# Favor attention and a feed-forward network on one core: the order of all engines, planned anew with measured durations

## The chip, the cores and the metric

The kernel runs on one core of one Trainium2 chip. The metric is the device time of one execution in microseconds (us). Before the change it is 939.01 us, the median of 3 runs (938.88 to 939.64).

## The reference

For 8 batches of 8 heads, 576 positions and head width 64, linear attention with 128 random features; its output, 4608 tokens by 512, goes through a feed-forward network 512 to 2048 to 512:

```python
def phi(x):
    proj = np.einsum('bhsd,md->bhsm', x, omega)
    h = proj - np.sum(x * x, axis=-1, keepdims=True) / 2.0
    return np.exp(h - np.max(h, axis=-1, keepdims=True)) / np.sqrt(m)
q_p, k_p = phi(q_s), phi(k_s)
kv, z = np.einsum('bhsm,bhsd->bhmd', k_p, v), np.sum(k_p, axis=2)
attn = np.einsum('bhsm,bhmd->bhsd', q_p, kv) / (np.einsum('bhsm,bhm->bhs', q_p, z)[..., None] + 1e-06)
x = attn.transpose(0, 2, 1, 3).reshape(B * S, H * D)
h = x @ w_in
out = (0.5 * h * (1.0 + erf(h / sqrt(2)))) @ w_out
```

## The kernel before, in words

**Attention.** The heads of a batch go in pairs, 4 units per batch, 32 in all. The first 8 units are computed in fp32, the 24 later ones from a high and a low part (`split_pre`, `split_post`). A unit's high part `r` is written by ScalarE (`x_high`, L979), and GpSimd writes the low part beside it (`x_low`, L984); both feed TensorE's projections (L992). Each batch has one scale group for v (`v_scales`, on GpSimd) that `v_a` and `v_b` need.

**Network.** The tokens go in 18 blocks of 256. Block 0 is plain fp32. In blocks 1 to 17 the first product is a Strassen-like scheme of seven products on fp16 high and low parts: `sw1` and `sw2` (`product`, L1264) for each of 8 chunks of hidden units, with the sums between by `comb_a` on ScalarE (L1271) and `comb_b`, `comb_c` on VectorE (L1276, L1277, L1282). Then `gelu` (L1290) and `g_high` (L1299) on ScalarE and `g_low` (L1364, writes `gl`) on VectorE, and the second product (`ffn_second`, L1374 to L1376) into `acc`; `o` leaves it by L1381 and L1383. In half of block 15 and in 16 and 17 the second product is Strassen-like too; its weight sums come late (`weights_out_sums`: L638, L649 on VectorE, L643 on GpSimd, L646 on ScalarE).

**Scales of a block.** Before a block's input can be split, `block_scales` computes its scale on GpSimd: six instructions of 32 x 1 elements (L505, L506, L507, L1215, L1216, L500), each needing one ahead of it. Blocks that span two batches take `be` from VectorE first (L1208). `block_spread` (L510, L511, ScalarE) copies the scale to the other partitions. Then `t_sum` (L1233, GpSimd, writes `ts`), `block_high` (L1243, ScalarE, writes `xh`) and `block_low` (L1246, VectorE, writes `xl`), four parts each, make what the block's products read. `gelu`, `g_high` and `g_low` read the scale tile too.

**The order.** All of it is decided when the program is built. Every step is an `op(engine, cost, function, ...)` with a planned duration in us. The class `Planner` (L234; its `run`, L280) plays the whole program through: whenever an engine is free in the plan, it takes, among the steps that are ready in the plan and have a buffer, the one with the lowest number in the table `RANK` (L37). The planner also keeps apart VectorE steps in the set `PORT` and steps of GpSimd. The order so found is fixed on each engine. Where the plan has TensorE waiting for more than 0.9 us, `put` (L1569) issues fill matmuls (L1574), whose result is overwritten:

```python
if X['fill'] and o.idle > 0.9 and o.t > 5.0:
    t = [G[k] for (_, k), name in zip(o.new, o.pick) if name in ANY]
    for _ in range(int((o.idle - 0.3) * X['fill'] / 0.11) if t else 0):
        nc.tensor.matmul(t[0][:, 0:256], id16[:, 0:P], id16, start=True, stop=True)
```

On the chip an engine runs its list in order and waits wherever an input is late, whatever the plan held.

Of the kernel before, what the change touches and what calls it, by code (L numbers as in the profile page):

```python
# [36 lines left out]
RANK = (0, 0, 0, 0, 0, 1, 2, 1, 4, 5, 1, 3, 1, 4, 2, 4, 7, 4, 5, 9, 8, 10, 9, 7, 13, 25, 28, 3, 10, 14, 12, 16, 13, 17, 17, 23, 19, 24, 22, 30, 23,  # L37
# [357 lines left out]
def favor_attention_ffn(ctx: ExitStack, tc: tile.TileContext, qT, kT, v, omT, w_in, w_out, out):  # L395
    nc = tc.nc
    B, H, D, S = qT.shape
    NJ = H // 2
    M = omT.shape[1]
    DM, F = w_in.shape  # L400
# [8 lines left out]
    NT = R2 // P  # L409
# [13 lines left out]
    cp = ctx.enter_context(tc.tile_pool(name="cp", bufs=1))  # L423
# [43 lines left out]
    op = PL.op  # L467
# [1145 lines left out]
```

## Time and profile before

| what | value |
|---|---|
| median of 3 runs | 939.01 us (938.88 to 939.64) |
| the profiled execution's own time | 938.51 us |
| its span | 936.5 us |
| mean granted TensorE clock | 0.995 |
| TensorE busy | 98% of the span |
| VectorE, ScalarE, GpSimd busy | 84%, 81%, 59% |
| DMA | 76 GB/s in the mean |

PE is TensorE's matmuls, PEld its weight loads (beside the matmuls), DVE VectorE, ACT ScalarE, POOL GpSimd. A row of a timeline gives start, duration, engine, line, operation, output<-input and size, and in brackets how long the engine stood idle just before and who released it. `[2.04 <-POOL bs L500]` reads: 2.04 us idle, ended when GpSimd's L500 had written `bs`. A row of the windows view gives the stretch, its length, busy time and count of PE, PEld, DVE, ACT and POOL, the granted clock of TensorE (1.00 is 2.4 GHz, 0.50 is 1.2 GHz), the busy share of DMA and its GB/s. A row of the waits view gives who waited for whom: total us, times, longest.

### The profile page before, as it was taken

What the parts mean: (1) busy time and instruction counts of PE and PEld (TensorE: products, weight loads), DVE (VectorE), ACT (ScalarE), POOL (GpSimd) and SP (SyncE); (2) the same over time, 40 slices, a digit from 0 to 9 for tenths busy, and PEclk for the clock granted to TensorE, in tenths of its full rate; (3) what the DMA queues carried; (4) which work ended last, traced back from release to release, by engine and by line L of the source; (5) the groups of instructions that cost most, each with busy time, mean ns of one, the idle gap of its engine ahead of it and who ended that gap; (6) DMA issues with size and microseconds to landing.
All of it is one profiled execution on the core that took longest, in us unless ns stands there. A gap on an engine that the chain in (4) does not pass through costs nothing.

```text
span 936.5 us, 26349 instructions
## 1 busy us (share of the span) xinstructions
PE 919.4 (98%) x10171; PEld 716.9 (77%) x10171; DVE 789.9 (84%) x2160; ACT 754.7 (81%) x1660; POOL 550.9 (59%) x809
## 2 busy tenths in 40 slices
PE   8999999999999999999999999999999999899998
PEld 7996777687767777777777777777777777679997
DVE  3777899999988998888988998899888998778764
ACT  5998988789979887979779897888898876657544
POOL 0454657747567664955466755674768744865432
PEclk8999999999999999999999999999999999999999
DMA  8884314033223232211221232112321100000000
GB/s 243 247 261 157 132 52 133 27 92 88 77 52 89 60 95 66 85 44 49 67 89 42 85 94 63 53 52 77 78 75 53 48 2 24 2 24 2 24 13 34
DMA packets 46316, 71.48 MB, mean 76 GB/s; under 512 B 13680, under 2 KB 22256, under 8 KB 46192
## 3 DMA queue, kind: packets, MB, share of 16 engines
q1 hardware_dynamic: 45824, 69.19, 24.7%
q8 instruction: 80, 1.31, 0.6%
q10 hardware_dynamic: 368, 0.62, 0.2%
q14 instruction: 44, 0.36, 0.1%
HBM read 60.36 MB, written 9.44 MB: 75 GB/s over the span
## 4 chain that ended last, share of the span: by engine, by line
PE 72%; DVE 12%; ACT 7%; POOL 4%; issue 2%; DMA 2%; SPq 1%; DVEq 0%; POOLq 0%; ACTq 0%
PE h L1264 25%; PE acc L1374 8%; PE acc L1375 8%; PE acc L1376 8%; PE h L1251 3%; PE acc L1367 3%; PE at L992 2%; PE at L1014 2%; PE at L1077 2%; PE at L864 2%; PE acc L1329 2%; PE at L1329 2%; DVE w L1067 1%; DVE h L1277 1%; DVE gl L1364 1%
## 5 line engine op out<-in xcount | busy, mean ns | idle before, releaser
L984 POOL TENSOR_TENSOR r<-xt,r 64x288 fp32r<-64x288 f32 (+2 forms) x216 | 164.8, 776 | 115.4 <-ACT r L979 85.8
L1264 PE MATMUL h<-xh,w 128*128 128x128 f16 x2176 | 219.5, 219 | 0.0
L1264 PE MATMUL h<-xl,w 128*128 128x128 f16 x1088 | 200.0, 219 | 0.0
L1264 PEld LDWEIGHTS <-w 128*128 128x128 f16 x3264 | 196.5, 98 | 4.5 <-issue 0.6
L1374 PE MATMUL acc<-woh,gh 128*128 128x512 f16 x448 | 170.5, 380 | 1.0 <-ACT o L1381 1.0
L1375 PE MATMUL acc<-woh,gl 128*128 128x512 f16 x448 | 170.0, 379 | 0.7 <-DVE gl L1364 0.6
L1376 PE MATMUL acc<-wol,gh 128*128 128x512 f16 x448 | 169.9, 379 | 0.0
L1264 PE MATMUL h<-xh,wih 128*128 128x128 f16 x816 | 156.9, 220 | 4.9 <-DVE gl L1364 2.5
L1264 PE MATMUL h<-xh,wil 128*128 128x128 f16 x816 | 156.1, 219 | 0.0
L1264 PE MATMUL h<-xl,wih 128*128 128x128 f16 x816 | 156.1, 219 | 0.0
L1264 PEld LDWEIGHTS <-wih 128*128 128x128 f16 x1632 | 139.3, 98 | 15.6 <-DVE h L1282 4.4
L1364 DVE SCALAR_TENSOR_TENSOR gl<-h,bs,gh 128x512 f16<-128x512 f32 x116 | 86.2, 744 | 18.9 <-ACT gh L1299 18.3
L1290 ACT ACTIVATE h<-h,bs 128x512 f32<-128x512 f32 x116 | 76.4, 660 | 24.7 <-PE h L1264 20.5
L979 ACT CAST r<-xt 128x256 fp32r<-128x256 f32 (+2 forms) x216 | 82.2, 407 | 8.2 <-PE at L992 3.5
L1264 PEld LDWEIGHTS <-wil 128*128 128x128 f16 x816 | 80.0, 98 | 10.1 <-issue 3.6
L1376 PEld LDWEIGHTS <-gh 128*128 128x128 f16 x464 | 45.4, 98 | 54.5
L1299 ACT ACTIVATE gh<-h,bs 128x512 f16<-128x512 f32 x116 | 79.8, 690 | 7.8 <-PE acc L1376 5.3
L1271 ACT COPY g<-h 128x256 f32<-128x256 f32 x136 | 50.4, 371 | 32.8 <-PE h L1264 30.6
L1375 PEld LDWEIGHTS <-gl 128*128 128x128 f16 x464 | 45.5, 98 | 37.4 <-DVE gl L1364 1.4
L1374 PEld LDWEIGHTS <-gh 128*128 128x128 f16 x464 | 45.3, 98 | 37.1
L1277 DVE TENSOR_TENSOR h<-h,g 128x256 f32<-128x256 f32 x136 | 58.8, 433 | 4.7
L589 POOL TENSOR_TENSOR w<-w 128x1024 int32<-128x1024 int32 x12 | 28.6, 2385 | 56.4 <-DVE w L583 25.9
(258 smaller groups left out, 2457.9 us busy)
## 6 DMA issues: line engine op xcount, KB each, us to landing
xt<-in_qT SPq DMA_DIRECT2D x56, 288.0 KB, 3.8
xt<-in_kT SPq DMA_DIRECT2D x54, 288.0 KB, 4.1
out_x<-o SPq DMA_DIRECT2D x35, 256.0 KB, 2.5
raw<-in_w_in SPq DMA_DIRECT2D x16, 512.0 KB, 5.8
raw<-in_w_out SPq DMA_DIRECT2D x16, 512.0 KB, 4.5
w<-in_v SPq DMA_DIRECT2D x24, 320.0 KB, 3.1
vt<-in_v SPq DMA_DIRECT2D x8, 320.0 KB, 5.1
xt<-in_kT ACTq DMA_DIRECT2D x2, 288.0 KB, 3.9
```

Of the source, the lines that this page charges most:

```text
L979: nc.scalar.copy(G['r', u, x][:, 0:b - a], xf[:, a:b])
L984: nc.gpsimd.tensor_tensor(r, xf[D:, a:b], r, op=ALU.subtract)
L1264: nc.tensor.matmul(h, w[p], x[r], start=first and i + m == 0, stop=last and i == 1 and m == 2, skip_group_check=True)
L1271: nc.scalar.copy(G['sa', n, c], G['h', n, c][:, 0:2 * P])
L1277: nc.vector.tensor_tensor(hv[:, 1:3], hv[:, 1:3], q.unsqueeze(1).broadcast_to([P, 2, P]), op=ALU.add)
L1290: nc.scalar.activation(h, h, AF.Gelu, scale=G['bs', n][:, 2:3])
L1299: nc.scalar.activation(G['gh', n, c], G['h', n, c], AF.Copy, scale=G['bs', n][:, 3:4])
L1329: nc.tensor.matmul(acc, a[x], b[y], start=first and m == 0, stop=False, skip_group_check=True)
L1364: nc.vector.scalar_tensor_tensor(G['gl', n, c], G['h', n, c], G['bs', n][:, 3:4], G['gh', n, c], op0=ALU.mult, op1=ALU.subtract)
L1374: nc.tensor.matmul(acc, gh, woh[:, f, c0:c1], start=f == 0, stop=False, skip_group_check=True)
L1375: nc.tensor.matmul(acc, gl, woh[:, f, c0:c1], start=False, stop=False, skip_group_check=True)
L1376: nc.tensor.matmul(acc, gh, wol[:, f, c0:c1], start=False, stop=f == NF - 1, skip_group_check=True)
```

## The change

It changes two things. The planned durations of some 27 steps are set to other values; the six-instruction scale group goes from 0.9 to 1.7 us, the group for v from 0.9 to 1.5. And the table `RANK` is another one. No step is added or taken out, and what each computes stays. Fill matmuls follow from the plan: 16 before, all at the program's start; 19 after, 15 at the start and 4 in the tail. The diff, cut to its core:

```diff
-RANK = (0, 0, 0, 0, 0, 1, 2, 1, 4, 5, 1, 3, 1, 4, 2, 4, 7, 4, 5, 9, 8, 10, 9, 7, 13, 25,
+RANK = (0, 0, 0, 0, 0, 1, 2, 1, 2, 5, 1, 3, 1, 4, 2, 2, 5, 4, 5, 9, 8, 10, 9, 6, 11, 10,
...
-        op('ACT', 1.14, w_hi, pc, w=[rk + ('hi',)], r=[rk])
-        op('ACT', 1.2, w_lo, pc, r=[rk], w=pc.lk if pc.l is not None else [rk + ('lo',)])
+        op('ACT', 1.04, w_hi, pc, w=[rk + ('hi',)], r=[rk])
+        op('ACT', 1.05, w_lo, pc, r=[rk], w=pc.lk if pc.l is not None else [rk + ('lo',)])
...
-        op('POOL', 0.9, v_scales, b, r=[('exp', b, 0)], new=[('vsc', ('vsc', b))])
+        op('POOL', 1.5, v_scales, b, r=[('exp', b, 0)], new=[('vsc', ('vsc', b))])
...
-                op('POOL', 0.2 + m / 455, x_low, u, x, r=xr, w=[rk])
+                op('POOL', 0.22 + m / 455, x_low, u, x, r=xr, w=[rk])
...
-        op('DVE', 1.06, v_b, u, r=[u.vk, ('vsc', u.b)], w=['vb'])
+        op('DVE', 0.81, v_b, u, r=[u.vk, ('vsc', u.b)], w=['vb'])
...
-        op('POOL', 0.9, block_scales, n, r=[('be', n), ('exp', b0, 1), ('wsc', 1)], new=[('bs', ('bs', n))], kind='B')
+        op('POOL', 1.7, block_scales, n, r=[('be', n), ('exp', b0, 1), ('wsc', 1)], new=[('bs', ('bs', n))], kind='B')
...
-        op('POOL', 0.21, block_out, n, r=[('bs', n), ('wsc', 0)], w=[('bo', n)])
+        op('POOL', 0.31, block_out, n, r=[('bs', n), ('wsc', 0)], w=[('bo', n)])
...
-            op('DVE', 0.31 + m / 940, block_low, n, p, r=[('bs', n), ('xh', n), ('xh', n, p)] + (ts or xr) + xt[1:] * (p > 0), w=[('xl', n, p)],
+            op('DVE', 0.12 + m / 940, block_low, n, p, r=[('bs', n), ('xh', n), ('xh', n, p)] + (ts or xr) + xt[1:] * (p > 0), w=[('xl', n, p)],
...
-        op('DVE', 0.65, comb_b, n, c, r=[('sa', n, c)], w=[hk], new=[('g', ('qs', n, c))], kind='F')
+        op('DVE', 0.77, comb_b, n, c, r=[('sa', n, c)], w=[hk], new=[('g', ('qs', n, c))], kind='F')
...
-        op('ACT', 0.66, g_high, n, c, r=[('bs', n), hk], new=[('gh', ('gh', n, c))], kind='F')
-        op('DVE', 0.71, g_low, n, c, r=[('bs', n), hk, ('gh', n, c)], new=[('gl', ('gl', n, c))], kind='F')
+        op('ACT', 0.6, g_high, n, c, r=[('bs', n), hk], new=[('gh', ('gh', n, c))], kind='F')
+        op('DVE', 0.66, g_low, n, c, r=[('bs', n), hk, ('gh', n, c)], new=[('gl', ('gl', n, c))], kind='F')
```

The other changed durations are of the same kind, most of them by 0.1 to 0.25 us. The order moves on all engines; three places follow. A number behind a name is that of the buffer and differs between the two programs.

**First place: GpSimd, where the scales of blocks 4 and 5 are made.** Before (`bs_4049` is block 4's scale, `bs_4075` block 5's, `vsc_4119` that of v for the next batch, `r_4145` a unit's low part):

```order
L500 TENSOR_SCALAR bs_4075<-bs_4075 32x1
L1224 TENSOR_TENSOR bs_4049<-bs_4049,wsc_81 128x1
L1224 TENSOR_TENSOR bs_4075<-bs_4075,wsc_81 128x1
L505 TENSOR_SCALAR vsc_4119<-vexp_80 32x1
L506 TENSOR_SCALAR vsc_4119<-vsc_4119 32x1
L507 TENSOR_SCALAR vsc_4119<-vsc_4119 32x1
L500 TENSOR_SCALAR vsc_4119<-vsc_4119 32x1 x2
L1233 TENSOR_TENSOR ts_4134<-xs_865 128x256
L1233 TENSOR_TENSOR ts_4134<-xs_865,ts_4134 128x256
L984 TENSOR_TENSOR r_4145<-xt_82,r_4145 64x256
```

After (`bs_4059` is block 4's scale; block 5's group follows only after the last row):

```order
L500 TENSOR_SCALAR bs_4059<-bs_4059 32x1
L1233 TENSOR_TENSOR ts_4105<-xs_883 128x256
L1233 TENSOR_TENSOR ts_4105<-xs_883,ts_4105 128x256 x2
L984 TENSOR_TENSOR r_4129<-xt_82,r_4129 64x256
L1233 TENSOR_TENSOR ts_4105<-xs_883 128x256
L505 TENSOR_SCALAR vsc_4165<-vexp_80 32x1
L506 TENSOR_SCALAR vsc_4165<-vsc_4165 32x1
L507 TENSOR_SCALAR vsc_4165<-vsc_4165 32x1
L500 TENSOR_SCALAR vsc_4165<-vsc_4165 32x1 x2
L984 TENSOR_TENSOR r_4179<-xt_82,r_4179 64x256
L984 TENSOR_TENSOR r_4185<-xt_82,r_4185 64x128
L984 TENSOR_TENSOR r_4183<-xt_82,r_4183 64x256
```

Three groups in a row have become one, then sums and a low part, then the group of v; block 5's group has moved behind three more low parts.

**Second place: ScalarE in the tail, around the scales of the last two blocks.** Before (`bs_12833` is block 14's scale, `bs_14530` block 17's):

```order
L1299 ACTIVATE gh_14483<-h_14323,bs_12833 128x512
L890 COPY xs_13532<-at_14459 128x64
L890 COPY xs_13532<-at_14402 128x64
L1271 COPY g_14496<-h_14371 128x256
L646 CAST w32_71<-et_83 128x1024
L510 COPY bs_14530<-bs_14530 32x5
L511 COPY bs_14530<-bs_14530 64x5
L1290 ACTIVATE h_14371<-h_14371,bs_12833 128x512
L1299 ACTIVATE gh_14569<-h_14371,bs_12833 128x512
```

After (`bs_12838`, `bs_14395`, `bs_14521`, `bs_14538` are the scales of blocks 14, 15, 16, 17):

```order
L1299 ACTIVATE gh_14476<-h_14322,bs_12838 128x512
L1243 ACTIVATE xh_14427<-ts_14304,bs_14395 128x512
L1290 ACTIVATE h_14358<-h_14358,bs_12838 128x512
L1299 ACTIVATE gh_14512<-h_14358,bs_12838 128x512
L646 CAST w32_71<-et_83 128x1024
L510 COPY bs_14521<-bs_14521 32x5
L511 COPY bs_14521<-bs_14521 64x5
L1243 ACTIVATE xh_14547<-xs_13363,bs_14521 128x256
L1243 ACTIVATE xh_14547<-xs_13363,bs_14521 128x512
L510 COPY bs_14538<-bs_14538 32x5
L511 COPY bs_14538<-bs_14538 64x5
L1383 ACTIVATE o_14565<-acc_13958,bs_12838 128x512
```

The last `gelu` and `g_high` of block 14 stood behind block 17's spread and now stand ahead of it; block 16's spread and first two high parts have come in between.

**Third place: VectorE in the tail.** Before (`xl_14366` is block 15's low part, of which the last two parts are shown):

```order
L1246 SCALAR_TENSOR_TENSOR xl_14366<-ts_14340,bs_14273,xh_14354 128x512
L1364 SCALAR_TENSOR_TENSOR gl_14494<-h_14323,bs_12833,gh_14483 128x512
L1276 TENSOR_TENSOR g_14499<-h_14371,g_14496 128x128
L1277 TENSOR_TENSOR h_14371<-h_14371,g_14499 128x256
L1282 TENSOR_TENSOR h_14371<-h_14371,g_14496 128x128
L1246 SCALAR_TENSOR_TENSOR xl_14366<-ts_14340,bs_14273,xh_14354 128x512
L638 TENSOR_TENSOR et_83<-woh_69,wol_70 128x1024
L649 TENSOR_TENSOR w32_71<-et_83,w32_71 128x1024
```

After (`xl_14478` is block 15's low part, `xl_14568` block 16's):

```order
L1246 SCALAR_TENSOR_TENSOR xl_14478<-ts_14304,bs_14395,xh_14427 128x512
L638 TENSOR_TENSOR et_83<-woh_69,wol_70 128x1024
L1364 SCALAR_TENSOR_TENSOR gl_14536<-h_14358,bs_12838,gh_14512 128x512
L649 TENSOR_TENSOR w32_71<-et_83,w32_71 128x1024
L1246 SCALAR_TENSOR_TENSOR xl_14568<-xs_13363,bs_14521,xh_14547 128x256
L1246 SCALAR_TENSOR_TENSOR xl_14478<-ts_14304,bs_14395,xh_14427 128x512
L1246 SCALAR_TENSOR_TENSOR xl_14568<-xs_13363,bs_14521,xh_14547 128x512
L1276 TENSOR_TENSOR g_14624<-h_14577,g_14621 128x128
```

Block 15's last low part, which its first product on TensorE reads, now stands behind the first low part of block 16. On TensorE the four new fill matmuls stand just ahead of that first product of block 15.

## Rows read from the trace of the kernel before

**Rows 1.** The page's first part: busy time, share, instructions of each engine.

```profile
PE 919.4 (98%) x10171; PEld 716.9 (77%) x10171; DVE 789.9 (84%) x2160; ACT 754.7 (81%) x1660; POOL 550.9 (59%) x809
```

**Rows 2.** Waits view, ScalarE's spreads waiting for GpSimd's block scales.

```profile
ACT bs L510 <- POOL bs L500: 8.7, 8, 2.7
```

**Rows 3.** Timeline at 270 to 280 us, GpSimd, ScalarE, TensorE.

```profile
272.94 0.18 POOL L505 TENSOR_SCALAR bs<-vexp 32x1 int32<-32x1 int32 x1
...
274.33 0.18 POOL L500 TENSOR_SCALAR bs<-bs 32x1 f32<-32x1 f32 x1
...
278.42 0.73 POOL L984 TENSOR_TENSOR r<-xt,r 64x256 fp32r<-64x256 f32 x1
...
274.55 0.20 ACT L510 COPY bs<-bs 32x5 f32<-32x5 f32 x1 [2.04 <-POOL bs L500]
...
279.20 0.50 PE L992 MATMUL at<-om,r 128*128 128x256 f32 x2 [0.98 <-POOL r L984]
```

**Rows 4.** Timeline at 385 to 388 us, ScalarE and TensorE.

```profile
385.78 0.19 ACT L510 COPY vsc<-vsc 32x3 f32<-32x3 f32 x1 [0.84 <-POOL vsc L500]
...
387.77 0.23 PE L1264 MATMUL h<-xh,wih 128*128 128x128 f16 x1 [0.68 <-DVE h L1282]
```

**Rows 5.** Timeline at 795 to 803 us, GpSimd, ScalarE, TensorE.

```profile
795.15 0.18 POOL L505 TENSOR_SCALAR bs<-be 32x1 int32<-32x1 int32 x1 [0.45 <-DVE be L1208]
...
797.48 1.05 POOL L500 TENSOR_SCALAR bs<-bs 32x1 f32<-32x1 f32 x1
...
800.22 0.20 ACT L510 COPY bs<-bs 32x5 f32<-32x5 f32 x1 [0.69 <-POOL bs L500]
...
802.18 0.22 PE L1264 MATMUL h<-xh,wih 128*128 128x128 f16 x1 [1.17 <-DVE gl L1364]
```

**Rows 6.** Timeline at 812 to 819 us, GpSimd, VectorE, ScalarE, TensorE.

```profile
812.02 0.51 POOL L505 TENSOR_SCALAR bs<-vexp 32x1 int32<-32x1 int32 x1
812.61 1.06 POOL L506 TENSOR_SCALAR bs<-bs 32x1 int32<-32x1 int32 x1
...
815.50 0.18 POOL L500 TENSOR_SCALAR bs<-bs 32x1 f32<-32x1 f32 x1
...
812.41 1.21 DVE L638 TENSOR_TENSOR et<-woh,wol 128x1024 f32<-128x1024 f16 x1
...
815.71 0.20 ACT L510 COPY bs<-bs 32x5 f32<-32x5 f32 x1 [2.70 <-POOL bs L500]
...
818.24 0.22 PE L1264 MATMUL h<-xh,wih 128*128 128x128 f16 x1 [1.36 <-DVE gl L1364]
```

**Rows 7.** Timeline of TensorE at five other places, rows with a wait.

```profile
147.49 0.38 PE L1374 MATMUL acc<-woh,gh 128*128 128x512 f16 x1 [0.97 <-ACT o L1381]
...
187.36 0.23 PE L1264 MATMUL h<-xh,wih 128*128 128x128 f16 x1 [0.93 <-DVE h L1282]
...
504.06 0.33 PE L880 MATMUL h<-ident,qh 128*128 128x128 f32 x1 [0.82 <-DVE gl L1364]
...
727.93 0.23 PE L1264 MATMUL h<-xh,wih 128*128 128x128 f16 x1 [0.49 <-DVE h L1282]
...
809.35 0.39 PE L1375 MATMUL acc<-woh,gl 128*128 128x512 f16 x1 [0.64 <-DVE gl L1364]
```

**Rows 8.** Timeline of TensorE at 814 us: block 15's first matmul.

```profile
814.04 0.22 PE L1264 MATMUL h<-xh,wih 128*128 128x128 f16 x1
```

**Rows 9.** Timeline of TensorE at 17 us: the longest wait of the start.

```profile
17.09 4.19 PE L817 MATMUL h<-vt,w 128*128 128x65 f32 x18 [2.41 <-DMA vt<-in_v]
```

**Rows 10.** Windows view, 16 to 24 us and 800 to 850 us.

```profile
16.00:24.00 8.00, 6.91 (x40) 6.32 (x42) 1.66 (x4) 4.87 (x14) 0.00 (x0) 0.57 0.66 185
800.00:850.00 50.00, 46.84 (x537) 34.52 (x536) 38.24 (x64) 29.50 (x56) 36.33 (x52) 1.00 0.03 12
```

More of the change, by code (lines that the diff above doesn't have):

```diff
@@ L32 @@
          pair=0, cp=0, qsp=1, klp=0, amax=0, qm=1, xm=0, km=0, prelu=1)
-RANK = (0, 0, 0, 0, 0, 1, 2, 1, 4, 5, 1, 3, 1, 4, 2, 4, 7, 4, 5, 9, 8, 10, 9, 7, 13, 25, 28, 3, 10, 14, 12, 16, 13, 17, 17, 23, 19, 24, 22, 30, 23,
[177 rows of a table removed]
+RANK = (0, 0, 0, 0, 0, 1, 2, 1, 2, 5, 1, 3, 1, 4, 2, 2, 5, 4, 5, 9, 8, 10, 9, 6, 11, 10, 14, 1, 9, 14, 11, 16, 13, 18, 17, 23, 19, 25, 22, 30, 23, 33,
[177 rows of a table added]
 PO = {}
@@ L700, in weights_in @@
         else:
-            op('DVE', 1.21, w_max, pc, r=bk, w=[('wmax', win, i)])
+            op('DVE', 1.14, w_max, pc, r=bk, w=[('wmax', win, i)])
     def weights_scale(win):
@@ L719, in weights_sums @@
         op('ACT', 0.68, a_high, c, r=[a, sc], w=[('ah', c)], kind='W')
-        op('DVE', 0.92, a_low, c, r=[a, sc, ('ah', c)], w=[('al', c)], kind='W')
+        op('DVE', 0.68, a_low, c, r=[a, sc, ('ah', c)], w=[('al', c)], kind='W')
         op('ACT', 0.46, a_high2, c, r=[b, sc], w=[('ah2', c)], kind='W')
@@ L725, in weights_sums @@
             op('ACT', 0.6, s_high, c, k, r=ts + [sc] + [('sh', c, 0)] * k, w=[('sh', c, k)] + [a] * (k == 0), kind='W')
-            op('DVE', 0.75, s_low, c, k, r=ts + [sc, ('sh', c, k)] + [('sl', c, 0)] * k, w=[('sl', c, k)] + [b] * (k == 0), kind='W')
+            op('DVE', 0.66, s_low, c, k, r=ts + [sc, ('sh', c, k)] + [('sl', c, 0)] * k, w=[('sl', c, k)] + [b] * (k == 0), kind='W')
     def weights_out_sums(c):
@@ L840, in bound @@
         op('ACT', 0.16, bound_a, u, r=[key, *more], new=[('zr', ('zr', u))])
-        op('DVE', 0.3, bound_b, u, r=[key], w=[('zr', u)], new=[('km', ('km', u))])
+        op('DVE', 0.26, bound_b, u, r=[key], w=[('zr', u)], new=[('km', ('km', u))])
         op('POOL', 0.31, bound_c, u, r=[('km', u), ('zr', u)], w=[('xm', u.b)])
@@ L919, in out_ops @@
                new=[(ANY if u.b == 0 else 'at', ('pn', u, hh))] + ([] if hh else [('dn', ('dn', u)), (('nx', 'qh') if u.split else 'nx', ('nx', u))]))
-            op('DVE', 0.85, norm, u, hh, r=[('pn', u, hh), ('dn', u), ('nx', u)] + vr, w=[('dn', u, hh), ('nx', u, hh)])
+            op('DVE', 0.88, norm, u, hh, r=[('pn', u, hh), ('dn', u), ('nx', u)] + vr, w=[('dn', u, hh), ('nx', u, hh)])
         for g in range(2):
@@ L1123, in chain @@
         op('DVE', 0.35, chain_b, b, x, r=[('cm',) + k], new=[('ct', ('ct',) + k), ('cg', ('cg',) + k)])
-        op('ACT', 0.5, chain_c, b, x, w=[('cg',) + k])
-        op('DVE', 0.15, chain_d, b, x, r=[('cg',) + k], w=[('exp',) + k])
+        op('ACT', 0.6, chain_c, b, x, w=[('cg',) + k])
+        op('DVE', 0.24, chain_d, b, x, r=[('cg',) + k], w=[('exp',) + k])
     def v_scales(b):
@@ L1169, in split_pre @@
                 op('DVE', 0.87, q_blocks, u, g, r=[('pp', u, i), ('mx', u)], w=es + [('mxg', u, g)])
-        op('POOL', 2.14, k_shift, u, r=[nm] + [nm + (i,) for i in range(NK)], w=[('et', u.eb, t) for t in range(NT)])
+        op('POOL', 2.19, k_shift, u, r=[nm] + [nm + (i,) for i in range(NK)], w=[('et', u.eb, t) for t in range(NT)])
         mx, mc, nq = ('mx', u), ('mc', u), ('nq', u)
@@ L1173, in split_pre @@
         op('ACT', 0.24, q_max, u, r=[mx] + [('mxg', u, g) for g in range(4)], new=[('mc', mc)])
-        op('DVE', 0.22, q_max2, u, r=[mc], w=[mx])
+        op('DVE', 0.12, q_max2, u, r=[mc], w=[mx])
         op('ACT', 0.22, q_max3, u, r=[mx], w=[mc])
@@ L1185, in split_post @@
         pk = ('pk', u)
-        op('ACT', 0.8, v_a, u, r=[u.vk, ('vsc', u.b), 'p2'], w=['vb'])
-        op('DVE', 1.06, v_b, u, r=[u.vk, ('vsc', u.b)], w=['vb'])
+        op('ACT', 0.74, v_a, u, r=[u.vk, ('vsc', u.b), 'p2'], w=['vb'])
+        op('DVE', 0.81, v_b, u, r=[u.vk, ('vsc', u.b)], w=['vb'])
         for g in range(len(KG)):
@@ L1197, in split_post @@
         op('ACT', 0.25, kv_c, u, r=[('kvz', u)], new=[('kvh', ('kvh', u))])
-        op('DVE', 0.45, kv_d, u, r=[('kvz', u), ('kvh', u)], new=[('kvl', ('kvl', u))])
+        op('DVE', 0.21, kv_d, u, r=[('kvz', u), ('kvh', u)], new=[('kvl', ('kvl', u))])
         bound(u, ('kvz', u), [('vsc', u.b)])
@@ L1202, in split_post @@
             op('ACT', 0.62, q_high, u, g, r=[('qt', u, g)] + ([('qf', u)] if g else []), w=[('qf', u, g)], new=[] if g else [('qf', ('qf', u))])
-            op('DVE', 0.74, q_low, u, g, r=[('qt', u, g), ('qf', u, g), ('qf', u)] + ([('ql', u)] if g else []), w=[('ql', u, g)], new=[] if g else [('ql', ('ql', u))])
+            op('DVE', 0.67, q_low, u, g, r=[('qt', u, g), ('qf', u, g), ('qf', u)] + ([('ql', u)] if g else []), w=[('ql', u, g)], new=[] if g else [('ql', ('ql', u))])
         out_ops(u)
@@ L1428, in ffn_first @@
                new=[] if p else [('h', hk)], due=(1, n, (c + p * .28) / NS, 0.0), kind='P')
-        op('ACT', 0.33, comb_a, n, c, r=[hk], new=[('g', ('sa', n, c))], kind='F')
-        op('DVE', 0.65, comb_b, n, c, r=[('sa', n, c)], w=[hk], new=[('g', ('qs', n, c))], kind='F')
-        op('POOL' if X['cp'] else 'DVE', 0.54 if X['cp'] else 0.28, comb_c, n, c, r=[('sa', n, c)], w=[hk, ('hb', n, c)], kind='F')
+        op('ACT', 0.28, comb_a, n, c, r=[hk], new=[('g', ('sa', n, c))], kind='F')
+        op('DVE', 0.77, comb_b, n, c, r=[('sa', n, c)], w=[hk], new=[('g', ('qs', n, c))], kind='F')
+        op('POOL' if X['cp'] else 'DVE', 0.54 if X['cp'] else 0.21, comb_c, n, c, r=[('sa', n, c)], w=[hk, ('hb', n, c)], kind='F')
         op('PE', 18 * .0558, sw2, n, c, r=ws + x + [(y, n, q) for y in ('xh', 'xl') for q in (1, 3)], w=[hk], due=(1, n, (c + .56) / NS, 0.0), kind='P')
@@ L1441, in ffn_first @@
                    new=[[('gh', ('gh', n, c))], [], [('rt', r)]][k])
-                op('DVE', (0.36, 0.36, 0.48)[k], h_low, n, c, k, r=[('bs', n), t, t + (k,), y] + [('gl', n, c)] * (k == 1) + [r] * (k == 2), w=[('hl', n, c, k)],
+                op('DVE', (0.46, 0.46, 0.54)[k], h_low, n, c, k, r=[('bs', n), t, t + (k,), y] + [('gl', n, c)] * (k == 1) + [r] * (k == 2), w=[('hl', n, c, k)],
                    new=[('gl', ('gl', n, c))] if k == 0 else [])
```

354 rows, old and new, of the table RANK are left out of this document.

## The prediction

> **What bounds the kernel now.** I read the page's busy shares first: TensorE is busy 919.4 of 936.5 us, 98% [rows 1], while the next engine, VectorE, stands at 84%. Nothing on the other engines costs time by itself, and TensorE's work is the same before and after but for three more fill matmuls. So a new order can only give back, or add, time in which TensorE waits. I then listed every wait of TensorE over 0.4 us in its timeline, looked up in the waits view who let it wait, and followed each back through the timelines of ScalarE, VectorE and GpSimd. Four chains lead to a scale group on GpSimd; five do not; one long wait stands in the start.
>
> **The waits that lead to scales.** An undisturbed scale group lasts from 272.94 to the end of its last row at 274.33 + 0.18, so 1.57 us [rows 3]. The plan of before held 0.9. In the tail two groups lasted longer still: 797.48 + 1.05 - 795.15 = 3.38 [rows 5] and 815.50 + 0.18 - 812.02 = 3.66 [rows 6]. An engine cannot go round a late scale, since its list is fixed, so ScalarE's spreads stood still eight times, 8.7 us together [rows 2]. What of it reaches TensorE:
> - At 272.94 the second of three groups in a row runs. ScalarE waits 2.04 us for it, and the unit's low part `r` comes off GpSimd only at 278.42; TensorE's projection waits for it 0.98 [rows 3].
> - At 385.78 ScalarE waits 0.84 for the group of v. What stands behind it is `comb_a`, whose late sum holds VectorE's `comb`, and TensorE waits 0.68 for that [rows 4].
> - At 800.22 ScalarE waits 0.69 for block 16's scale, right behind block 15's; `gelu` and `g_high` stand behind that, `gl` comes late, TensorE waits 1.17 [rows 5].
> - At 815.71 ScalarE waits 2.70 for block 17's scale, with the last `gelu` and `g_high` of block 14 behind it; TensorE waits 1.36 for the `gl` that follows [rows 6].
>
> Together 0.98 + 0.68 + 1.17 + 1.36 = 4.19 us.
>
> **The change part by part.** *Durations.* No duration does anything on the chip; they only shape the order. The 1.7 us fits the undisturbed 1.57 and still falls short of the tail's 3.38 and 3.66. *First place.* The three groups in a row are split: block 5's and the one of v no longer stand ahead of the low parts that TensorE wants first, so what held `r` is gone: 0.98 saved. What would be late next is the scale of block 5; it is read only by that block's high and low parts, which stand behind it on the lists, and GpSimd has 41% of its time free [rows 1]. At 385 us the same holds for v: planned longer, its group is asked for later, 0.68 saved. *Second place.* Block 14's last `gelu` and `g_high` now stand ahead of block 17's spread, so that wait of ScalarE no longer delays `gl`: 1.36 saved whatever the group lasts. Block 16's group has moved behind GpSimd's sums and weight sums, and its spread behind that same `g_high`: 1.17 saved. *Third place: a new wait.* Block 15's last low part on VectorE stands behind the first of block 16, and that needs block 16's scale and ScalarE's first high part of block 16. If the scale is late, everything behind it on VectorE is late too, and TensorE's first product of block 15 waits for it. Before, that product started without a wait [rows 8]. That a wait is there now is also read from the four fill matmuls in front of it, since the code puts them only where the plan has TensorE idle for over 0.9 us. Its cost on the chip is not in the trace of before. From below it is 0 [rows 8]; a gain there is excluded, because there was no wait to remove. From above I take the longest wait for any one input, 2.41 us [rows 9]. The nearest rows are the tail's own, 1.17 and 1.36, and the 0.97 and 0.98 elsewhere [rows 5, 6, 7, 3]: I take **1.0**. Should the wait be absent, the fills themselves cost something like it: four of 256 columns at, at most, half of the 0.50 that two such matmuls take, 1.0 [rows 3]. *All else.* I cost the other moved steps at nothing: they move within lists that run beside TensorE, and what covers them is the slack of 16 to 41% on the other engines [rows 1]; where that cover fails, the result is the second rival. DMA issues move along with their steps, but the start, where the one wait for a transfer lies [rows 9], has the same transfers ahead of that matmul; it stays.
>
> Sum against the profiled execution: 938.5 - 4.2 + 1.0 = 935.3 us. The median of the runs lies 0.5 above that execution (939.01 against 938.51), so I forecast **935.8 us**. With the bounds 0 and 2.41 the forecast's own range is 934.8 to 937.2.
>
> **A rule against the trace.** In the tail one of the group's instructions took 1.06 us, and it ran while VectorE had a 1.21 us instruction with two inputs from SBUF [rows 6]; the same kind took 0.18 at 272.94 and at 274.33 [rows 3]. The Trainium skill (SBUF — State Buffer, section Who interferes with whom) says that a VectorE instruction with two SBUF inputs and a GpSimd instruction that reads SBUF exclude each other for the whole instruction. The trace agrees, with 1.06 in place of 0.18. By the rows two or three of the six were caught, and the group grew by 2.1 at most; by the rule all six could be, an estimate of 6 x 0.88 = 5.3 us, and the sum would be 935.3 + 5.3 = 940.6 if all of it reached block 15. That is the direction of the third rival, which is priced from rows alone and has its chance.
>
> **The rivals.**
> - *All waits go (chance 0.13).* The five other waits, 0.97 + 0.93 + 0.82 + 0.49 + 0.64 = 3.85 us [rows 7], vanish too, and no new one comes: 938.5 - 4.19 - 3.85 = 930.5, plus 0.5, **931.0**. For it: other durations were set right too, `v_b` and `comb_b` among them, on which the waits at 187 and 727 hang. Against it: the fills say that the new plan itself holds a wait, and none of these five has a scale group near it.
> - *The waits only change place (0.21).* The change then does not do what it says: ten thousand instructions were put in another order, and each list can wait in new spots. For it: five of the nine waits had nothing to do with scales [rows 7], so wrong scale durations were not the main source of waits; and tail groups last twice the new 1.7. Then the new waits come to the old 4.2, and the time is **939.0**, 938.5 to 939.5.
> - *Slower: block 16's scale, stretched, holds block 15 and the clock (0.16).* In the new tail the scales of 16 and 17 run on GpSimd just where VectorE has its two-input instructions. If block 16's group is stretched as block 17's was, it takes 3.66 in place of 1.57, 2.1 more, and all of it falls on the chain scale, high part, low part of 16, low part of 15, first product: a wait of 1.0 + 2.1 = 3.1. After the wait of 2.41 in the start the granted clock stood at its lower level: in the 8 us from 16 on its mean was 0.57 [rows 10], which is 8 x (1 - 0.57) = 3.4 us lost if TensorE would have been busy all along. After the 1.17 and 1.36 of the tail it stayed at 1.00 [rows 10]. So it decides from a wait like that at 17.09 on: 938.5 - 4.2 + 3.1 + 3.4 = 940.8, plus 0.5, **941.3**. Below that point the wait alone gives 937.9, and the result counts with no change. For it: both tail groups of before were stretched. Against it: a group beside which VectorE has no such instruction takes 1.57 [rows 3], and the fills keep TensorE busy for part of the wait.
>
> **How the numbers follow.** The forecast gets 0.50, because three of its four savings are seen in the lists themselves. A measurement of this kernel can tell about 0.2%, 1.9 us, from no change: the bounds are 937.1 and 940.9. Faster by more: forecast and first rival, 0.63. Within: the second, 0.21. Slower by more: the third, 0.16. The range runs from 931.0 to 941.3: that leaves out half of the first rival and half of the third, some 0.15 together.
>
> **What would show it.** Right: ScalarE's wait for block scales falls from 8.7 us to under 4; no wait of TensorE at `r` behind two scale groups; no `gl` wait of over 1 us in the tail; TensorE's idle time before block 15's first matmul, fills counted, near 1 us; clock 1.00 there. Wrong: the waits of TensorE over 0.4 us again sum to 8 us at other lines (second rival); over 2.4 us idle ahead of block 15 and a granted clock under 0.9 in the windows after it (third rival); or a start that is longer, which no term here covers.

## The result, and the profile after

The changed kernel takes 929.12 us (median of 4 runs, 927.4 to 929.78) beside 938.94 us before (4 runs, 935.33 to 939.64). The ratio is 0.9896, with a 95% interval of 0.9877 to 0.9914: 9.8 us faster, where 3.2 us had been forecast, and below the range. The profiled execution took 929.59 us, its span is 927.4, so 9.1 us less than the span of before.

The runs of one kernel differ by up to 5 us, and their mean granted clock goes with that: of 11 further runs of before, taken beside the first experiments, the one at 1.000 took 935.73 us, the one at 0.994 took 940.04. With the lost part (1 - clock) x span taken off each run ("the clock's loss" from here on), the 11 runs come to a median of 935.1 us and the four of the changed kernel to 927.7. So about 7.4 us belong to the order and the rest to the clock, of which more below. This is good to about 1 us: the mean clock also counts a fall behind TensorE's last matmul, which delays no matmul (0.9 us of the loss in the profiled execution of before, none in that of the changed kernel).

First the page's busy shares and, from the waits view, the rows that answer to [rows 1] and [rows 2], with TensorE's longest waits (total us, times, longest):

```profile
PE 915.4 (99%) x10174; PEld 715.6 (77%) x10174; DVE 789.2 (85%) x2160; ACT 752.6 (81%) x1658; POOL 560.1 (60%) x809
```

```profile
PE h L1264 <- DVE h L1282: 3.6, 3, 1.3
PE h L817 <- DMA vt<-in_v: 2.5, 1, 2.5
...
PE h L1264 <- ACT xs L890: 0.5, 1, 0.5
...
ACT bs L510 <- POOL bs L500: 4.8, 3, 2.0
```

ScalarE waits for block scales three times instead of eight, and all three lie in the tail, at 796, 804 and 808 us. TensorE's timeline, at the places of [rows 3 to 8] as far as anything is left there:

```profile
188.06 0.23 PE L1264 MATMUL h<-xh,wih 128*128 128x128 f16 x1 [1.04 <-DVE h L1282]
...
703.31 0.22 PE L1264 MATMUL h<-xh,wih 128*128 128x128 f16 x1 [0.54 <-ACT xs L890]
...
807.34 0.60 PE L1574 MATMUL h<-ident 128*128 128x256 bf16 x4
807.78 0.22 PE L1264 MATMUL h<-xh,wih 128*128 128x128 f16 x1
...
811.63 0.27 PE L1264 MATMUL h<-xh,w 128*128 128x128 f16 x2
811.74 0.22 PE L1264 MATMUL h<-xl,w 128*128 128x128 f16 x1
813.18 0.23 PE L1264 MATMUL h<-xh,wih 128*128 128x128 f16 x1 [1.22 <-DVE h L1282]
...
816.70 0.23 PE L1264 MATMUL h<-xh,wih 128*128 128x128 f16 x1 [1.33 <-DVE h L1282]
```

No wait is left at 279, 387, 147, 504 or 802. One stays at 188; at 727 none is left, but one at 703, ended by another step (L890), is about as long as that was; and two new ones stand at 813 and 817. Block 15's first product, at 807.78, has none: the four fills ahead of it take 0.44 us (807.34 to 807.78), and no input is late.

**A wait costs more than its bracket.** The matmul at 811.74 lasts 0.22 us, but the next starts 0.06 later when nothing is late: the two at 811.63 take 0.11 until 811.74. At 813.18 the bracket says 1.22, while from start to start 1.44 passed, 1.38 more than undisturbed: 0.16 us of a wait are not shown, since the bracket begins only where the earlier matmul's 0.22 us end. After 100 us the trace of before has 14 waits of TensorE over 0.1 us with 8.9 us in brackets, so 8.9 + 14 x 0.16 = 11.2 us; the changed kernel has 5 with 4.3, so 5.1. Counted from start to start, wait by wait, the two traces give the same 11.2 and 5.1. That is 6.1 of the 9.1 us.

The start, for [rows 9] and [rows 10]:

```profile
17.48 0.74 PE L817 MATMUL h<-vt,w 128*128 128x65 f32 x5 [2.52 <-DMA vt<-in_v]
```

```profile
16.00:24.00 8.00, 6.52 (x54) 5.75 (x56) 3.08 (x8) 5.44 (x14) 0.19 (x1) 0.79 0.71 186
```

The wait for v is as long as before (2.52 against 2.41), but the mean clock of these 8 us is 0.79, not 0.57: 8 x (1 - 0.79) = 1.7 us lost in place of 3.4. Block 1's first product starts 1.75 us earlier than before (118.00 against 119.75). From there to the end the span is 809.4 us against 816.8, and 6.1 of these 7.4 are the waits above; of the last 1.3, 0.2 lie behind TensorE's last matmul (4.2 us of span are left there before, 4.1 after), and for the others no single place is known.

### The profile page after: what moved, and what is told of

Same layout as the page of the kernel before. It is cut to its first block, busy times and chain, and to the rows that moved or that the text cites. A ratio compares the mean times of both kernels' runs of the same rounds, so it can differ in the third digit from the quotient of the medians.

```text
span 927.4 us, 26371 instructions
## 1 busy us (share of the span) xinstructions
PE 915.4 (99%) x10174; PEld 715.6 (77%) x10174; DVE 789.2 (85%) x2160; ACT 752.6 (81%) x1658; POOL 560.1 (60%) x809
## 4 chain that ended last, share of the span: by engine, by line
PE 93%; POOL 2%; DVE 2%; DMA 1%; SPq 1%; ACT 1%; issue 1%; DVEq 0%
PE h L1264 32%; PE acc L1374 10%; PE acc L1375 10%; PE acc L1376 10%; PE h L1251 3%; PE acc L1367 3%; PE at L1014 3%; PE at L992 3%; PE acc L1329 3%; PE at L864 2%; PE at L1077 2%; PE at L1329 2%; PE at L854 1%; PE at L880 1%; DMA vt<-in_v 1%; PE at L817 1%
## 5 line engine op out<-in xcount | busy, mean ns | idle before, releaser
L984 POOL TENSOR_TENSOR r<-xt,r 64x256 fp32r<-64x256 f32 (+2 forms) x216 | 169.4, 797 | 116.1 <-ACT r L979 79.6
L979 ACT CAST r<-xt 128x256 fp32r<-128x256 f32 (+2 forms) x216 | 84.1, 406 | 21.9 <-PE at L992 10.9
L1271 ACT COPY g<-h 128x256 f32<-128x256 f32 x136 | 50.4, 370 | 31.7 <-PE h L1264 30.5
L992 PE MATMUL at<-om,r 128*128 128x256 f32 x216 | 52.9, 336 | 0.0
```

What stands on the lines that cost most here:

```text
L979: nc.scalar.copy(G['r', u, x][:, 0:b - a], xf[:, a:b])
L984: nc.gpsimd.tensor_tensor(r, xf[D:, a:b], r, op=ALU.subtract)
L992: nc.tensor.matmul(o[:, t], r[:, t * P:(t + 1) * P], om, start=True, stop=True)
L1271: nc.scalar.copy(G['sa', n, c], G['h', n, c][:, 0:2 * P])
```

## The experiments

**Durations and table apart.** Theory 1: the right durations carry the gain. Theory 2: a table fits only the durations it was annealed under, that is, under which it was searched for. Theory 3: the table alone carries it.

```diff
e1_durations_only, against the changed kernel
-RANK = (0, 0, 0, 0, 0, 1, 2, 1, 2, 5, ...   (the change's table)
+RANK = (0, 0, 0, 0, 0, 1, 2, 1, 4, 5, ...   (the table of before)
e2_table_only, against before
-RANK = (0, 0, 0, 0, 0, 1, 2, 1, 4, 5, ...
+RANK = (0, 0, 0, 0, 0, 1, 2, 1, 2, 5, ...
e3_scales_only, against before
-        op('POOL', 0.9, v_scales, ...
+        op('POOL', 1.5, v_scales, ...
-        op('POOL', 0.9, block_scales, ...
+        op('POOL', 1.7, block_scales, ...
e4_all_but_scales, against the changed kernel: the same two lines put back to 0.9
```

> All durations of the change, with the table RANK of before. Before 938.9 us, changed kernel 929.1. Theory 1 (the right durations carry the gain, above all those of the scale groups): the planner delays what it now knows to be late, most waits go, 931 to 934. Theory 2 (a table fits only the durations it was annealed under; the gain is that of the pair): the old table under new durations is as good as unsearched, new waits appear, 938 or above. Theory 3 (the table alone carries it): no gain, 938 to 940.

> The table RANK of the change, with all durations of before. Theory 1: the plan holds the wrong 0.9 us for scales again, ScalarE waits over 6 us for block scales, 935 to 939. Theory 2: 938 or above, for the table meets durations that it was not annealed under. Theory 3 (the table alone carries it): 929 to 931.

> The kernel before with two durations set anew, those of the scale groups (0.9 to 1.7 and 0.9 to 1.5 us), the old table. Theory 1: the four waits of TensorE behind scales (4.2 us of idle time) go and the five others stay, about 935. Theory 2: those waits go, but the order from there on is another one that nobody searched, with new waits of 2 to 6 us, 936 to 941.

> The changed kernel with the two durations of the scale groups put back to 0.9 us, everything else new. Theory 1 (scales above all): the gain is lost by about its larger half, 934 to 936, with waits of ScalarE for block scales back at 7 us or more. Theory 2: lost too, 934 or above, but with waits at lines that have no scale near. Rival: the other durations carry the gain, 929 to 931.

| kernel | median us | ratio to before, 95% | median with the clock's loss off | waits of TensorE over 0.1 us after 100 us |
|---|---|---|---|---|
| before | 938.66 | | 935.1 | 14, 8.9 us |
| durations only | 954.63 | 1.019 (1.0166 to 1.0214) | 949.6 | 27, 18.0 us |
| table only | 956.03 | 1.0191 (1.017 to 1.0213) | 952.2 | 30, 20.4 us |
| scales only | 947.77 | 1.0102 (1.0082 to 1.0122) | 941.7 | 18, 12.5 us |
| all but scales | 947.36 | 1.0099 (1.008 to 1.0118) | 941.3 | 21, 15.5 us |

All four are slower than before, each by 8.7 us or more, and by 6.2 or more with the clock's loss off. Theories 1 and 3 fall, and theory 2 holds more strongly than it was put: two durations set nearer to the measured ones, and nothing else, cost 9.1 us (scales only), although the waits they were set for did shrink: in its waits view ScalarE's spreads wait 1.3 us for block scales, not 8.7. (In all but scales they wait 5.1; 7 or more had been expected.) Part of the new waits is in the plans themselves, as the fills show, which stand only where the plan has TensorE idle: 29, 32 and 35 in the first three kernels, 16 before (all but scales has 15). New waits of TensorE stand where there was none, such as this one in scales only:

```profile
301.85 0.23 PE L1264 MATMUL h<-xh,wih 128*128 128x128 f16 x1 [2.59 <-DVE gl L1364]
```

So an edited plan gives another order from the first moved step on, and nobody has searched that one. What a duration is worth can't be read from such a pair. It needs the order held fixed. The opposite pair is missing: no run has a new table searched under the old durations, so how much of the change's gain a new search alone would have found stays open.

**The order held fixed, the chip changed to fit the plan.** The kernel before keeps each list; the scale groups are made about as short as the plan held them (in its trace one goes from 370.01 to 370.95, 0.94 us). What is left out are the products behind the first three instructions; constants stand in their place, so this kernel serves to measure time and its output is not the reference's.

```diff
     def block_scales(n):
...
-        fields(G['be', n] if b1 > b0 else vexp[:, 1, b0:b0 + 1], b[0:32], TOPX)
+        short(G['be', n] if b1 > b0 else vexp[:, 1, b0:b0 + 1], b[0:32], TOPX, 5)
...
-        nc.gpsimd.tensor_tensor(b[0:32, 2:3], b[0:32, 1:2], wsc[0:32, 1, 2:3], op=ALU.mult)
-        nc.gpsimd.tensor_scalar(b[0:32, 3:4], b[0:32, 0:1], wsc[0:32, 1, 1:2], 1.0 / z, op0=ALU.mult, op1=ALU.mult)
-        mul(nc.gpsimd, b[0:32, 4:5], b[0:32, 2:3], z)
+    def short(e, sc, top, n):
+        fields(e, sc, top); nc.gpsimd.tensor_scalar(sc[:, 2:n], sc[:, 0:1].broadcast_to([32, n - 2]), 0.0, 1e-9, op0=ALU.mult, op1=ALU.add)
```

> The kernel before, order unchanged, with the scale groups cut to four instructions each (the products with the weights' scales and, for v, one product by a constant are left out, constants stand there), so that a group takes about the 0.9 to 1.05 us that the plan of before held. Theory A (the plan's wrong duration made the waits): the four waits behind scales go, 4.8 us, about 934; the five others stay. Rival: the waits come from other durations or from the tail's VectorE instructions, and at least two of the four stay: 936 to 939.

931.83 us (6 runs), ratio 0.9928 (0.9907 to 0.9949); with the clock's loss taken off 928.1 beside 934.9, so 6.8 us. Its waits of TensorE over 0.1 us after 100 us are 7 with 3.8 us, at 0.16 more each 4.9 beside 11.2. Theory A had 4.8: it is right in the main, and too small. Of its profile, TensorE's waits view and the rows left in the tail:

```profile
PE h L817 <- DMA vt<-in_v: 2.1, 1, 2.1
PE h L1264 <- DVE gl L1364: 1.1, 2, 0.7
PE h L525 <- DVE w L516: 1.1, 1, 1.1
PE acc L1374 <- ACT o L1381: 1.0, 1, 1.0
PE acc L1375 <- DVE gl L1364: 0.8, 1, 0.8
PE h L1264 <- DVE h L1282: 0.8, 2, 0.6
```

```profile
802.12 0.39 PE L1375 MATMUL acc<-woh,gl 128*128 128x512 f16 x1 [0.77 <-DVE gl L1364]
...
810.37 0.22 PE L1264 MATMUL h<-xh,wih 128*128 128x128 f16 x1 [0.73 <-DVE gl L1364]
```

The waits at 279, 387 and 802 are gone, as theory A says (the row at 802.12 here is the wait that stood at 809). That at 818, here at 810, is only halved: in the tail the short group too is stretched, from 804.78 to 807.80, 3.0 us. Gone with them are those at 504 and 727, which the prediction had put among the five that do not lead to scales. The one at 147 (`o` L1381) stays, the one at 187 falls from 0.93 to 0.56.

The rival to this reading is that four instructions are simply less work. So the same cut was made in the changed kernel, whose plan held the long group.

> The changed kernel with the scale groups cut to four instructions, as in the run that did the same to the kernel before (there 931.8 beside 938.6; the same parts left out, constants in their place). Theory A (what counts is whether plan and chip agree): this order was planned for 1.7 us, so a shorter group only comes early; it can help in the tail alone, where the group is stretched: 0 to 2.5 us less than 929.1. Rival (the four instructions are simply less work for GpSimd and VectorE): a gain of about 6.8 us here too, 922 to 924.

930.36 us (5 runs), ratio to before 0.991 (0.9886 to 0.9934), beside 929.91 for the changed kernel unedited in the same series. No gain clear of the noise: for this order less work is worth nothing in the sum. It is not without effect, since in its profile the wait at 813 is gone and a new one stands at 726:

```profile
726.02 0.23 PE L1264 MATMUL h<-xh,wih 128*128 128x128 f16 x1 [1.47 <-DVE h L1282]
```

So the 6.8 us are what short groups give to an order that was planned for short groups, and not what four instructions cost less than six.

**Two places alone.**

```diff
kernel before, lists kept; moved:
+POOL: block_scales(5), block_out(5) behind x_low((3, 1), 3)
+ACT:  block_spread(5), block_high(5, 0) behind x_high((3, 1), 4)
+ACT:  gelu(14, 7), g_high(14, 7) ahead of block_spread(17)
```

> The kernel before, every list as it was, with two places alone edited as the change edits them: block 5's scale group, its spread and first high part moved behind two more low parts, and block 14's last gelu and g_high ahead of block 17's spread. Theory A (a wait behind a scale can be taken away where it stands): no wait of TensorE at 279 and none of over 0.5 us at 818; each wait is worth its idle time and 0.16 us more, 1.14 + 1.52 = 2.7 us, so 936.0 beside 938.7. Theory B (what is gained at a place is given back at the next): 938 to 939, with a new wait within 20 us of each place.

939.79 us (12 runs), ratio 1.001 (0.9991 to 1.0028): no gain, where theory A had 2.7 us. The second place did as theory A says: the 1.36 us at 818 are gone, with 0.27 at 831 in their stead. At the first, theory B is right: the wait at 279 is gone, and the late scale, met further on, costs more.

```profile
285.62 0.20 ACT L510 COPY bs<-bs 32x5 f32<-32x5 f32 x1 [2.67 <-POOL bs L500]
...
291.90 0.38 ACT L1271 COPY g<-h 128x256 f32<-128x256 f32 x1
```

```profile
292.32 0.23 PE L1264 MATMUL h<-xh,wih 128*128 128x128 f16 x1 [2.52 <-ACT g L1271]
```

From the spread on ScalarE has no idle time; behind it stand, among others, the unit's high parts and then two `comb_a` (L1271), for the second of which TensorE waits 2.52. In this profile the granted clock then falls too, to 0.57 in the mean of the 4 us from 292 on, so 1.7 us more are lost:

```profile
292.00:296.00 4.00, 3.68 (x31) 3.54 (x32) 2.83 (x10) 2.23 (x6) 3.76 (x4) 0.57 0.44 139
```

This edit put the spread where the scale was still late; it speaks for how little a single list can be moved by hand there.

**The start.** Sixteen fills before the matmul that waits for v, in the kernel before:

```diff
+        for _ in range(16 if o.fn is kv and o.a[0] is units[1] else 0):
+            nc.tensor.matmul(G['pk', units[1]][:, 0:256], id16[:, 0:P], id16, start=True, stop=True)
         o.fn(*o.a)
```

> The kernel before with 16 fill matmuls more, in the start, ahead of the matmul that waits 2.4 us for v. Theory C (TensorE's idle time there lets the clock fall, and that is what differs from run to run): the granted clock stays at 1.00 in the windows from 16 to 24 us, mean clock 0.999 to 1.000 in every run, the median falls by the 3 to 4 us that a mean clock of 0.996 costs, to about 935. Rival (the clock falls for another reason, or at another wait): clock 0.996 as before, 938 to 940.

```profile
17.21 0.44 PE L817 MATMUL h<-vt,w 128*128 128x65 f32 x2 [0.63 <-DMA vt<-in_v]
```

```profile
16.00:24.00 8.00, 7.37 (x78) 6.19 (x76) 4.08 (x7) 7.01 (x20) 1.40 (x1) 1.00 0.69 190
```

The wait falls to 0.63, the clock stays at 1.00, and all 12 runs have a mean clock of 0.999 or 1.000. Theory C holds for the clock. The median is 937.09, ratio 0.9981 (0.9967 to 0.9995): 2.5 us less than the 939.57 of before in that series, where the clock's loss is 3.8 (935.8 with it off). About 1 us of these 3.8 can be the fall behind the last matmul, which this kernel's profile has as well (1.0 us) and which costs nothing. Whether the fills themselves cost anything can't be told from these runs.

> The changed kernel once more, nothing edited, beside the others of this call. Its four runs so far had a mean clock of 0.998 to 1.000, those of before 0.994 to 1.000. If the clock of the start is chance, the new runs have 0.994 to 1.000 too and a median of 928 to 931; if the changed start protects it, 0.998 or more in each, 927.4 to 929.8.

929.91 us (5 runs), clocks 0.996, 0.997, 0.998, 1.000, 1.000: the first case, since a single run of the changed kernel can lose as much as many of before. But it is not chance alone. Its nine runs have a mean of 0.9984, the 45 of before that stand beside the experiments 0.9967; none of the nine is at 0.995 or below, 11 of the 45 are. So by mean clock the changed kernel loses some 1.6 us less on average. In the profiled pair the clock stood at its lower level for 3.4 us in place of 6.8 after waits of like length, as in the second profile of the changed kernel. What in the order does this is not shown.

**Can it be made faster still?** With the lists of the changed kernel kept, single steps were moved at the waits that are left. The chain at 813 reads as follows, ScalarE and then VectorE:

```profile
808.17 0.20 ACT L510 COPY bs<-bs 32x5 f32<-32x5 f32 x1 [2.02 <-POOL bs L500]
...
808.62 1.26 ACT L1383 ACTIVATE o<-acc,bs 128x512 f32<-128x512 f32 x2
809.77 0.37 ACT L1271 COPY g<-h 128x256 f32<-128x256 f32 x1
```

```profile
810.18 0.29 DVE L1276 TENSOR_TENSOR g<-h,g 128x128 f32<-128x128 f32 x1 [2.42 <-ACT g L1271]
810.50 0.43 DVE L1277 TENSOR_TENSOR h<-h,g 128x256 f32<-128x256 f32 x1
811.18 1.73 DVE L638 TENSOR_TENSOR et<-woh,wol 128x1024 f32<-128x1024 f16 x1 [0.25 <-POOL et L643]
812.84 0.28 DVE L1282 TENSOR_TENSOR h<-h,g 128x128 f32<-128x128 f32 x1
```

Block 15's first `comb` starts late behind block 17's scale, and its last step (L1282), which TensorE waits for, stands behind a weight-sum step of 1.73 us that nothing near waits for.

```diff
changed kernel, lists kept; e7_after_tail moves:
+DVE: comb_c(15, 0) ahead of o_both(5); comb_c(15, 2) ahead of o_low(4)
+ACT: comb_a(15, 2) ahead of block_high(16, 2); block_spread(17) behind store(14, 1)
e8_after_all_waits, besides:
+DVE: comb_b(2, 2), comb_c(2, 2) ahead of v_max((2, 3))
+ACT: put_x((6, 2), 1) ahead of chain_c(6, 1)
-        if X['fill'] and o.idle > 0.9 and o.t > 5.0:
+        if X['fill'] and o.idle > 0.9 and 5.0 < o.t < 100.0:
e12_after_waits_and_start, besides: the 16 fills of the start, and
+ACT: comb_a(15, 1) ahead of o_high(4); gelu(15, 0), g_high(15, 0) ahead of block_high(16, 2)
+DVE: comb_b(15, 1), comb_c(15, 1) ahead of o_both(5); g_low(15, 0) ahead of o_low(4)
```

> The changed kernel, every list as it is, with four steps moved in the tail: block 15's first and third comb_c ahead of a weight-sum step on VectorE each, its third comb_a ahead of a high part that waits for GpSimd's sums, block 17's spread behind two stores. Theory A: the two tail waits of TensorE (1.2 and 1.3 us idle, 1.4 and 1.5 with what the idle time does not show) hang on these, 2.9 us less than the changed kernel's 929.1, about 926.5. Theory B: block 16's parts come late in their place, a wait of 1 us or more at 818 to 845, 928 to 929.

> As the run before, and three steps moved at the two other waits of the changed kernel (block 2's third comb ahead of a maximum on VectorE at 187, a copy out of the h buffer ahead of six small copies on ScalarE at 703), and the four fill matmuls of the tail left out. Theory A: 2.9 + 1.2 + 0.7 + 0.4 = 5.2 us less than 929.1, about 924. Theory B: the waits come back at other lines, 927 to 929.

> The changed kernel with the moves of the run with all waits edited, six more of the same kind in the tail (block 15's second comb and its first gelu, g_high and g_low ahead of the weight sums' steps or of a high part that waits), no fills in the tail and the 16 fills in the start. Theories A and C together: the waits of 1.5 and 0.6 us that were left in the tail fall to under 0.8 in all, clock 0.999 or more in every run, 923.5 to 924.5, with less spread than any kernel so far. If a moved step makes block 16 late instead, 925 to 927.

| kernel | median us (runs) | ratio to before, 95% | median with the clock's loss off |
|---|---|---|---|
| changed | 929.12 (4), 929.91 (5) | 0.9896, 0.9907 | 927.7, 928.1 |
| tail moves | 929.37 (6) | 0.9906 (0.988 to 0.9932) | 927.0 |
| all moves | 926.02 (5) | 0.9882 (0.9856 to 0.9908) | 926.0 |
| all moves, start filled | 926.94 (5) | 0.9883 (0.9857 to 0.9908) | 926.3 |

The tail moves take 2.55 us of brackets in the tail to 1.59 but bring a wait for GpSimd of 1.18 us at 236.56 that the profile of the changed kernel lacked; the changed kernel's second profile has the same one (1.16 at 234.57), so it comes and goes and is not the edit's. All moves together beat both kernels by the median, 3 us under the changed kernel and 12.5 under before; about half of these 3 us is the clock, which differs from run to run, and the intervals of the two ratios overlap, so a gain over the changed kernel is not shown. In its profile the waits at 188 and 703 are gone but for 0.83, and the tail still waits:

```profile
PE h L1264 <- DVE h L1282: 1.5, 1, 1.5
PE h L1264 <- DVE gl L1364: 1.4, 2, 0.8
PE h L817 <- DMA vt<-in_v: 1.3, 1, 1.3
```

A move takes only a part of what its wait was worth (1.04 to 0.83 at 188): the next late input stands close behind. The six further moves took the tail's longest wait from 1.5 to 0.85, and the start's fills gave clocks of 0.999 and 1.000; the time did not fall with them. All three kernels are slower than was expected of them: 926.5, 924 and 923.5 to 924.5 us. In the last the tail still waits 1.7 us in brackets where under 0.8 had been expected.

## Why the prediction was wrong

- **Right:** what bounds the kernel, that only TensorE's waits can change, and that wrong scale durations were the main source of them. ScalarE's waits for block scales fell from 8.7 to 4.8 us; under 4 had been expected. The waits at 279 and 387 went.
- **The step that failed: "five do not" (lead to a scale group).** The prediction followed a wait to its releaser and one or two steps beyond, and left 3.85 us standing because no scale group was near. The run with short groups shows that the waits at 504 and 727 hang on them too (by which path at 504 is open). At 727 the chain is plain in the trace of before, on ScalarE and then VectorE, one step further back than was read:

```profile
723.68 0.20 ACT L510 COPY bs<-bs 32x5 f32<-32x5 f32 x1 [0.79 <-POOL bs L500]
...
724.72 0.36 ACT L1271 COPY g<-h 128x256 f32<-128x256 f32 x1
```

```profile
725.11 0.29 DVE L1276 TENSOR_TENSOR g<-h,g 128x128 f32<-128x128 f32 x1 [1.64 <-ACT g L1271]
```

  The spread waits for a scale, `comb_a` behind it is late, VectorE's `comb` too; from there VectorE is busy without a break, and the next `comb`, behind this one, is what TensorE waits for 2.8 us later. In the changed kernel the waits at 147 and 504 are gone as well (0.97 + 0.82 in brackets), that at 187 stays (0.93, then 1.04), and the one at 703 is new in the place of that at 727; which part of the change freed the one at 147, which short groups do not free, no run tells apart.
- **Mis-sized: the price of a wait.** The sum took the brackets. Each wait costs 0.16 us more, so 14 of them 2.2 us more; and five of 0.13 to 0.23, 0.9 in brackets and 1.7 in all, were left out as too small. All five went.
- **The tail: a saving and a cost at the wrong lines.** "1.36 saved whatever the group lasts" failed: block 17's late spread no longer holds `gelu` and `g_high`, but it holds `comb_a` (2.02 us, the chain at 813 above), and TensorE waits 1.22 for what follows. Before, the waits there were 1.17 + 0.64 + 1.36 = 3.2 in brackets; after, 0.14 + 1.22 + 1.33 = 2.7, and 0.44 of fills (estimated at up to 1.0). So of the 2.5 us to be saved nothing was saved, as the third rival's first half says: the groups of blocks 16 and 17 take 3.6 and 3.5 us there (804.36 + 0.18 - 800.92, and 807.96 + 0.18 - 804.62), not 1.57:

```profile
800.92 0.24 POOL L505 TENSOR_SCALAR bs<-vexp 32x1 int32<-32x1 int32 x1
...
802.58 1.70 POOL L1216 TENSOR_SCALAR bs<-bs,wsc 32x1 f32<-32x1 f32 x1
804.36 0.18 POOL L500 TENSOR_SCALAR bs<-bs 32x1 f32<-32x1 f32 x1
804.62 0.18 POOL L505 TENSOR_SCALAR bs<-vexp 32x1 int32<-32x1 int32 x1
...
807.96 0.18 POOL L500 TENSOR_SCALAR bs<-bs 32x1 f32<-32x1 f32 x1
```

  The new wait of 1.0 did not come at block 15's first product, whose low part was in time behind block 16's, but twice further on, at the `comb` steps. The net of the tail is 0 where the prediction had -2.5 + 1.0 = -1.5. The third rival's clock did not fall: no wait of the tail reached the 2.4 us of the start, and the clock of 800 to 850 us stayed at 1.00.
- **Not in the sum: the clock of the start**, which differs from run to run. "It stays", said of the start, was right of the wait and wrong of its price: 1.7 us in the profiled executions, about as much on average, by no step that the prediction had foreseen.
- The rule of the Trainium skill that was weighed there (SBUF — State Buffer, section Who interferes with whom) agrees with the trace: with VectorE's low parts and weight-sum steps beside them, instructions of the scale group that take 0.18 to 0.25 elsewhere took up to 1.70 (L1216 at 802.58). The two groups took 3.6 and 3.5 us, more like the rows' 3.66 than the estimate's 1.57 + 5.3.

Taken by these steps, forecast -3.2: the tail adds 1.5, the waits at 188 and 703, a little longer than those at 187 and 727, 0.2; the two places at 279 and 387 with their 0.16 each take 0.3, the waits at 147 and 504 take 2.1, the short ones 1.7, the start's clock 1.7, and 1.7 have no known place (the 1.3 of above, and the 0.4 by which the tail's fills work against it). That is -9.0 beside the -9.1 of the two spans.

## What to carry to other kernels

When an order comes out of a plan, find the step whose planned duration the trace contradicts: holding the order fixed and making that step as short as planned told its worth (6.8 us), while editing the plan without a new search made every kernel slower by 8.7 us or more. Follow a wait of the bottleneck back until a releaser is itself not late, since a late step was found up to three engines away from the wait it made. And compare runs with their granted clock beside them before a difference of a few us is explained.

## What was not expected of the hardware

- The clock of the start: in every profiled execution whose wait at 17 us was 1.8 us or longer the granted clock then stood at its lower level for some 3 to 10 us; in the three with 0.6 to 1.3 us there it stayed at 1.00. In kernels without the fills that wait, mostly for one transfer of v, came out between 1.3 and 3.2 us. The length of a wait does not settle it alone: in mid-program the clock fell after the wait of 2.52 us at 292 (two places alone) and stayed at 1.00 after that of 2.59 at 301 (scales only).
- An instruction of 32 x 1 elements on GpSimd (L1216), 0.25 us in each of the 17 groups before, took 1.70 us beside VectorE's steps of 128 x 512 and 128 x 1024.
